# Three tiles in place of two for the pre-mix's input, and clearing split between VectorE and GpSimd

## The chip, the cores and the metric

The kernel runs on one core of one Trainium2 chip. The metric is device time in microseconds (us). One execution of the kernel before is profiled; times elsewhere are of separate runs. Engines are called PE (TensorE), ACT (ScalarE), DVE (VectorE), POOL (GpSimd) and SP (SyncE, which only issues transfers).

## The reference

Attention whose heads are mixed before and after the softmax, then two feed-forward layers, all in float32. 4 batches, 12 heads, 448 positions, 64 columns a head.

```python
scores = scale * np.matmul(q, k.transpose(0, 1, 3, 2))
scores = np.einsum('bhij,hg->bgij', scores, w_pre)       # pre-mix of the heads
scores = scores - np.max(scores, axis=-1, keepdims=True)
attn = np.exp(scores)
attn = attn / (np.sum(attn, axis=-1, keepdims=True) + 1e-09)
attn = np.einsum('bhij,hg->bgij', attn, w_post)          # post-mix
out = np.matmul(attn, v)
...
x = out.transpose(0, 2, 1, 3).reshape(B * S, H * D)      # 1792 x 768
x = elu(x @ moe_w_in) @ moe_w_out                        # 768 -> 2048 -> 768
h = x @ moe2_w_in                                        # 768 -> 1024
x = layernorm(h * softmax(h)) * g_ln @ moe2_w_out        # 1024 -> 768
```

## The kernel before

The attention goes through 17 chunks of query rows (`CH`, line 24). A chunk has G slots (4, 8, 12, 12, 9 in the first batch; 9 to 12 later), and a slot holds 10 query rows of all 12 heads. Two slots make a unit; there are 90.

For a chunk the steps are these. **Scores** (line 443): for each pair of heads PE multiplies queries by keys into PSUM tiles `sc`. **Eviction** (line 449): ACT or DVE copies each head's scores into an SBUF tile `sev` (8 buffers; `s` for chunk 0). **Moves** (lines 451 to 454): 13 DMAs bring the rows of the 12 heads into one tile `sp`, so that heads lie on partitions: head h of query row a on partition 13a + h. **Pre-mix** (line 510): one matmul of `wpre_t` with a slot of `sp` into `pm` (3 PSUM buffers, a unit uses two). Then follow for each unit the maximum on DVE (`st`, line 515), the exponential with its sum on ACT (`e`, 520), the division folded into the post-mix weights (`wr`, 531), the **post-mix** (`po`, 543), and its copy to `at` (551). When a chunk is complete, `av` (592) multiplies by the values, and the result goes to DRAM (`xs`).

`sp` has two tiles of 128 x 12 x 448 float32. They lie in the pools `spa` (right end of SBUF) and `spb` (left), and chunk c uses tile (17 - c) % 2. So the moves of chunk c wait until the pre-mix of chunk c-2 has read its last slot. Rows of the tile that no move writes must be zero, so both tiles are cleared whole at the start, one by DVE and one by POOL (line 470); DVE also clears the two PSUM tiles `po` (472), and POOL scales `wpre_t` (466).

The keys lie in a ring `k` of 12 buffers on the right side, behind `spa`; a batch needs 6. When the attention is near its end, `start_moe` (662) gives back `sev`, `q`, `kst`, `k` and `spa` and lays the tiles of the feed-forward layer there.

The order on every engine is made by a planner at build time. Each step is an `op` (287) with a rank (a due time in us), what it depends on, ring buffers that it takes (`bufs`, 284), and an estimated duration for each engine that may do it. `schedule` (296) simulates the engines: it takes the engine that could start first and, of the steps that it could then start, that with the lowest rank, and emits it. The engines run what they were given in order and wait on semaphores; SP, too, issues its transfers in order. `lag` is the time that the planner reckons from the end of a DMA's issue to the landing: 3.5 us for a move.

The due times: units' pre-mixes and post-mixes stand one behind the other from T0 = 14 us on (`plan_front`, lines 360 to 389). The scores of chunk c >= 2 are spread evenly between the first pre-mix of chunk c-1 (`lo`) and the first pre-mix of chunk c less SCM = 12 us (`hi`), lines 390 to 393. Steps on SP may be planned up to 4 us ahead of their rank (`AHS`), others up to 100 us (`AHD`). The moves of chunks 0 and 1 may be issued by SP or ACT, those of chunk 2 by SP or POOL, all others by SP.

The feed-forward layers behind (from line 725 on) are ordered by hand in their own loops and do not pass through the planner.

Of the kernel before, what the change touches and what calls it, by code (L numbers as in the profile page):

```python
# [9 lines left out]
F32 = mybir.dt.float32  # L10
# [4 lines left out]
ALU = mybir.AluOpType  # L15
# [3 lines left out]
NB, NH, S, D = 4, 12, 448, 64  # L19
# [4 lines left out]
CH = [(b, 10 * sum(n[:i]), n[i]) for b in range(NB) for n in [[[4, 8, 12, 12, 9], [11, 12, 12, 10], [12, 12, 12, 9], [11, 12, 12, 10]][b]] for i in range(len(n))]  # L24
NC = len(CH)
# [12 lines left out]
XB = 2  # L38
# [12 lines left out]
DB = .9  # L51
DA = .2
T0 = 14
SCM = 12
KD = 3.5
VD = 28
WB = 3
SB = 8
VB = 2
EB = 10  # L60
LEAD = 3

@with_exitstack
def kernel(ctx: ExitStack, tc: tile.TileContext, qa, kt, vt, wpre, wpost,
# [4 lines left out]
    nc = tc.nc  # L69
    ctx.enter_context(tc.manual_schedule())  # L70
    pools = {}

    def pool(name, bufs=1, side="left", space=None):
        kw = {"space": space} if space is not None else {"side": side}
        p = tc.alloc_tile_pool(name=name, bufs=bufs, reuse_waits="tile", **kw)
        pools[name] = p
        return p

    def release(*names):
        for n in names:  # L80
            pools.pop(n).release()
# [44 lines left out]
    wpre_t = const.tile([128, 64], F32, name="wpre_t")  # L126
    wpost_t = const.tile([128, 60], F32, name="wpost_t")

    pool("spa", 1, "right")
    k_p = pool("k", 12, "right")  # L130
    kst_p = pool("kst", 2, "right")
    q_p = pool("q", 4, "right")
    sev_p = pool("sev", SB, "right")
# [145 lines left out]
    class Op:  # L279
# [2 lines left out]
    ops = []  # L282
    tail = {"pe": .3, "act": .2, "dve": .17, "pool": .1, "sp": 2.0, "host": 0.0}
    bufs = {"sc": 3, "pm": 3, "po": 2, "sev": SB, "e": EB, "wr": WB, "st": 4, "kst": 2, "q": 4,
            "k": 12, "sp0": 1, "sp1": 1, "at": 2, "v": VB, "x": XB, "ws": 4, "wy": 2}

    def op(rank, emit, deps=(), new=(), uses=(), more=0.0, lag=None, **us):

        o = Op()
        o.rank, o.emit, o.deps, o.new, o.us, o.more, o.lag = rank, emit, [d for d in deps if d is not None], new, us, more, lag  # L290
        for b in chain(new, uses):
            b.users.append(o)
        ops.append(o)
        return o

    def schedule():
        free = dict.fromkeys(tail, 0.0)
        rings = {r: [] for r in bufs}
        todo = sorted(ops, key=lambda o: o.rank)

        def seen(o, e):

            if o.lag is not None:
                return o.end + o.lag
            if o.eng == e and e not in ("sp", "dve"):
                return o.end
            return o.end + tail[o.eng] + o.more

        def ready(o, e):
            t = 0.0  # L310
            for d in o.deps:
                if d.end is None:
                    return None
                t = max(t, seen(d, e))
            more = dict.fromkeys(bufs, 0)
            for b in o.new:
                ring = rings[b.ring]
                n = bufs[b.ring] - more[b.ring]
                more[b.ring] += 1
                if b.at is None and len(ring) >= n:  # L320
                    for u in ring[-n].users:
                        if u.end is None:
                            return None
                        t = max(t, seen(u, e))
            return t

        while todo:
            cand, start = [], {}
            for o in todo[:WIN]:
                opts = []  # L330
                for e, us in o.us.items():
                    r = ready(o, e)
                    if r is None:
                        break
                    r = max(r, o.rank - (AHS if e == "sp" else AHD))
                    opts.append((max(r, free[e]) + us + (DB if e == "dve" and "pool" in o.us and o.rank > TD else DA if e == "dve" and "act" in o.us else 0.0), r, e))
                else:
                    _, r, e = min(opts)
                    cand.append((o, e, r))
                    start[e] = min(start.get(e, 1e9), max(r, free[e]))  # L340
            e = min(start, key=start.get)
            o, _, r = min((c for c in cand if c[1] == e and c[2] <= start[e] + GRACE), key=lambda c: c[0].rank)
            o.eng = e
            t = max(r, free[e])
            o.end = free[e] = t + o.us[e]
            for b in o.new:
                if b.at is None:
                    b.at = o
                    rings[b.ring].append(b)
            o.emit(e)  # L350
            todo.remove(o)
        return max(free.values())
# [9 lines left out]
    t, nf, t_hid = T0, 0, None  # L362
# [32 lines left out]
    kt_t, kb, q_t, qb_, sp_t, sp_op, pre_op, e_t = {}, {}, {}, {}, {}, {}, {}, {}  # L395
# [3 lines left out]
    def dma(out, in_, e="sp"):  # L399
        {"act": nc.scalar, "pool": nc.gpsimd, "sp": nc.sync}[e].dma_start(out=out, in_=in_)  # L400
# [27 lines left out]
    def add_score(c, h):  # L428

        b, _, G = CH[c]  # L430
        n = 5 * G
        ring = ("sc", "pm")[h // 2 % 2] if c == 0 else "sc"
        scb, svb = [Buf(ring) for _ in range(2)], [Buf("sev") for _ in range(2)]
        r = t_sc[c, h]
        key = "sc", c, h

        def mm(e):
            T[key] = [pools["ps_" + ring].tile([128, 512], F32, tag=ring, name="sc") for _ in range(2)]
            q, k = q_t[c, h // 6], kt_t[b, h]
            for x in range(2):  # L440
                for i in range(2):
                    sl = slice(64 * i, 64 * i + 64)
                    nc.tensor.matmul(T[key][i][64 * x:64 * x + 64, :S], q[sl, h % 6 // 2, 64 * x:64 * x + 64], k[sl, :],  # L443
                                     start=True, stop=True)

        def evac(e, i):
            t = T["sv", c, h + i] = (k0.tile([128, S], F32, name=f"s0_{h + i}") if c == 0 else
                                     sev_p.tile([128, S], F32, tag="sev", name="sev"))
            copier(e)(t, T[key][i][:, :S])  # L449

        def move(e, i, p, r0, r1):
            if c not in sp_t:
                sp_t[c] = sp_t[c - 2]
            dma(sp_t[c][p:p + 13 * (r1 - r0 - 1) + 1:13, 0:G, :], T["sv", c, h + i][r0 * G:r1 * G], e)

        o1 = op(r, mm, [k_op[b, h], q_op[c, h // 6]], scb, [qb_[c, h // 6], kb[b, h]], pe=SC)
        for i in range(2):
            sv = [] if c == 0 else [svb[i]]
            o2 = sc_ev[c, h + i] = op(r + .9 + .1 * i, lambda e, i=i: evac(e, i), [o1], sv, [scb[i]], act=.43, dve=.54)
            for n, to in enumerate([(h + i, 0, 10)] if h + i < 11 else [(11, 0, 5), (64, 5, 10)]):  # L460
                sp_op.setdefault(c, []).append(op(r + 2 + .2 * i + .1 * n, lambda e, i=i, to=to: move(e, i, *to), [o2], [spb_[c]], sv, lag=3.5, sp=.78, **({"act": .78} if c < 2 else {"pool": 1.0} if c == 2 else {})))

    spb_ = {c: Buf(f"sp{(NC - c) % 2}") for c in range(NC)}
    o = op(7.0, lambda e: dma(wpre_t, wpre), sp=.5)
    o_wpost = op(T0 + 2, lambda e: dma(wpost_t, wpost), sp=.5)
    w_op = op(T0 - 8, lambda e: nc.gpsimd.tensor_scalar(wpre_t, wpre_t, 0.125, None, ALU.mult), [o], pool=.6)

    for c in range(2):
        sp_t[c] = pools["spb" if (NC - c) % 2 else "spa"].tile([128, NH, S], F32, tag="sp", name="sp")
        (nc.gpsimd if c else nc.vector).memset(sp_t[c], 0.0)  # L470
    for t in po_p:
        nc.vector.memset(t, 0.0)

    def begin(e):
        release("k0")
# [21 lines left out]
    for u, sl in enumerate(units):  # L497
# [62 lines left out]
        o = op(r0 + 3.2, guard, ex, [], [sb], dve=.07)  # L560
        o = op(r0 + 3.3, inv, [o], [], [sb], dve=.07)
        ow = op(r0 + 3.4, weigh, [o, o_wpost], [wb], [sb], dve=.3, pool=.38)
        r0 = t_post[u]
        o = op(r0, post, ex + [ow], pob, eb + [wb], pe=POST)
# [5 lines left out]
    for c in range(NC):  # L570
# [12 lines left out]
        for n in range(2):  # L583
            r = t_av[c, n]
# [10 lines left out]
            o = op(r, mm, at_ops[c] + ov, [avb], [vb, at_b[c]], pe=AV * w / 120)  # L595
# [10 lines left out]
            o = op(r + AV + .2, take, [o], [xb], [avb], act=.36, dve=.42)  # L606
# [4 lines left out]
    for n in range(16):  # L611
# [40 lines left out]
        o = op(t0, load, [last], [sb], sp=.5, lag=11.0)  # L652
        o = op(t0 + 4, clamp, [o], [], [sb], dve=.17)
        oa = op(t0 + 4.5, scale, [o], [], [sb], act=.26)
        o = op(t0 + 5, loword, [o], [], [sb], dve=.17)
        o = op(t0 + 5.5, sign, [o], [], [sb], dve=.27)
        o = op(t0 + 6, join, [oa, o], [], [sb], dve=.27)
# [3 lines left out]

    def start_moe(e):
        nonlocal gln_t
        release("sev", "q", "kst", "k", "spa")
        p = pool("wstg", 2, "right")
        gln_t = p.tile([128, F2 // 128], F32, name="gln_t", bufs=1)
        dma(gln_t, gln)
        w1_alloc(0, pool("w1a", 1, "right"))
        xT_alloc(0, pool("xT0", 1, "right"))
# [43 lines left out]
    for ft in range(2):  # L713
        o = None
# [3 lines left out]
    for i in range(3):  # L718
        ws = Buf("ws")
# [252 lines left out]
```

## Time and profile before

| | us |
|---|---|
| median of 3 runs | 1096.0 (1095.16 to 1097.95) |
| profiled execution, its time | 1094.9 |
| its span, first to last instruction | 1093.1 |
| PE busy in the span | 1059.9 (97%) |
| DVE, ACT, POOL busy | 722.0, 504.2, 231.6 |
| mean granted clock of PE | 0.998 |

The first pre-mix begins at 17.85 us and the last one at about 356 us; behind that comes the feed-forward part. Busy time of PE is an upper bound of its useful time, since ends of matmuls are modelled. What stands in brackets in a timeline row is the idle time of that engine just before, and what ended it.

### The profile page before, as it was taken

The numbers are of one execution on the slowest core, as the hardware profiler recorded it, in microseconds if no ns is written. First come the engines' busy times: TensorE is split into PE (matmuls) and PEld (weight loads), VectorE is DVE, ScalarE is ACT, GpSimd is POOL, SyncE is SP. The second block draws the span as 40 slices with busy tenths as digits, with TensorE's granted clock in tenths as the row PEclk, the third lists the DMA queues.
The fourth block names the chain that finished last, engine by engine and source line by source line (L and its number), as shares of the span: only waits on it lengthen the run. The fifth ranks groups of instructions, "written<-read, shape, count | busy, mean of one in ns | idle before, by whom it ended". The sixth has DMA issues, their size and how long they took to land.

```text
span 1093.1 us, 28427 instructions
## 1 busy us (share of the span) xinstructions
PE 1059.9 (97%) x11800; PEld 888.6 (81%) x11800; DVE 722.0 (66%) x1391; ACT 504.2 (46%) x1071; POOL 231.6 (21%) x243
## 2 busy tenths in 40 slices
PE   6899999999999999999999999999999999999998
PEld 2457667667666898998988999999999889898988
DVE  6576687677677557687887887878864644353522
ACT  3566676677676455333333443333431434342422
POOL 2211010011011325343343433343431000000000
PEclk9999999999999999999999999999999999999999
DMA  6875775775746442415234242423262400000001
GB/s 200 210 209 172 216 238 172 219 221 176 232 149 197 132 133 72 155 58 171 99 117 149 83 154 77 140 91 126 70 243 100 194 30 15 30 23 22 30 15 44
DMA packets 80287, 141.69 MB, mean 130 GB/s; under 512 B 20853, under 2 KB 59969, under 8 KB 80157
## 3 DMA queue, kind: packets, MB, share of 16 engines
q1 hardware_dynamic: 78345, 136.59, 39.1%
q10 hardware_dynamic: 1332, 2.09, 0.6%
q8 instruction: 93, 1.52, 0.6%
q0 software_dynamic: 480, 1.19, 0.4%
q14 instruction: 37, 0.30, 0.1%
HBM read 75.96 MB, written 25.17 MB: 93 GB/s over the span
## 4 chain that ended last, share of the span: by engine, by line
PE 74%; DMA 9%; DVE 8%; ACT 4%; issue 2%; SPq 1%; POOL 1%; ACTq 0%; DVEq 0%; POOLq 0%
PE h L256 15%; PE o L745 15%; PE o L888 11%; PE h L841 11%; PE av L592 6%; PE sc L443 5%; PE pm L510 5%; PE po L543 5%; DMA sp<-sev 3%; DMA ws<-in_wo_dram 2%; DVE x L761 1%; DVE wy L184 1%; DMA ws<-in_wi_dram 1%; PE tr L872 1%; DVE wq L180 1%
## 5 line engine op out<-in xcount | busy, mean ns | idle before, releaser
L520 ACT ACTIVATE e<-pm,st 128x448 f32<-128x448 f32 x180 | 113.4, 635 | 72.3 <-DVE st L515 65.9
L515 DVE TENSOR_REDUCE st<-pm 128x1 f32<-128x448 f32 x180 | 105.1, 617 | 60.9 <-PE pm L510 58.6
L745 PE MATMUL o<-gh,woh 128*128 128x448 f32 x384 | 141.3, 368 | 3.8 <-ACT x L759 1.9
L745 PE MATMUL o<-glo,woh 128*128 128x448 f32 x384 | 139.9, 364 | 0.0
L745 PE MATMUL o<-gh,wol 128*128 128x448 f32 x384 | 139.8, 364 | 0.0
L443 PE MATMUL sc<-kt,q 64*64 64x448 f32 x816 | 123.8, 565 | 9.7 <-ACT sev L449 4.6
L543 PEld LDWEIGHTS po<-wr,e 60*64 60x64 f32 x5040 | 102.4, 135 | 37.0 <-issue 23.8
L269 POOL TENSOR_TENSOR glo<-g,gh 128x448 fp32r<-128x448 f32 x64 | 83.1, 1298 | 217.9 <-issue 124.5
L510 PE MATMUL pm<-sp,wpre_t 64*64 64x448 f32 x720 | 112.2, 558 | 10.4 <-DMA xs<-x 4.4
L888 PE MATMUL o<-w,lh 128*128 128x384 f32 x448 | 120.3, 340 | 0.0
L543 PE MATMUL po<-wr,e 60*64 60x60 f32 x5040 | 109.1, 219 | 2.3 <-issue 1.1
L841 PE MATMUL h<-w,x2h 128*128 128x512 f32 x336 | 107.7, 395 | 0.0
L761 DVE TENSOR_TENSOR x<-x,o 128x448 f32<-128x448 f32 x168 | 101.4, 610 | 7.9 <-PE o L745 7.9
L256 PE MATMUL h<-xh,wih 128*128 128x448 f32 x288 | 105.5, 366 | 0.0
L256 PE MATMUL h<-xh,wil 128*128 128x448 f32 x288 | 105.0, 365 | 0.0
L256 PE MATMUL h<-xl,wih 128*128 128x448 f32 x288 | 104.9, 364 | 0.0
L264 ACT ACTIVATE t<-t 128x448 f32<-128x448 f32 x64 | 37.0, 578 | 134.7 <-DVE t L263 134.7
L531 POOL TENSOR_TENSOR wr<-wpost_t,st 128x120 f32<-128x120 f32 x90 | 36.3, 403 | 294.7 <-DVE st L527 225.7
L592 PEld LDWEIGHTS av<-at,v 128*64 128x64 f32 x1632 | 75.8, 137 | 14.1 <-DVE st L515 3.5
L592 PE MATMUL av<-at,v 128*64 128x120 f32 (+5 forms) x1632 | 83.2, 258 | 3.3 <-issue 1.8
L745 PEld LDWEIGHTS o<-gh,woh 128*128 128x128 f32 x384 | 72.1, 188 | 12.7 <-DVE x L761 4.5
L888 PEld LDWEIGHTS o<-w,lh 128*128 128x128 f32 x448 | 81.7, 188 | 0.6
(98 smaller groups left out, 1930.2 us busy)
## 6 DMA issues: line engine op xcount, KB each, us to landing
sp<-sev SPq DMA_DIRECT2D x94, 210.0 KB
ws<-in_wi_dram SPq DMA_DIRECT2D x33, 512.0 KB
ws<-in_wo_dram SPq DMA_DIRECT2D x21, 512.0 KB
q<-in_qa_dram SPq DMA_DIRECT2D x34, 192.0 KB
v<-in_vt_dram SPq DMA_DIRECT2D x24, 256.0 KB
w2s<-ws SPq DMA_DIRECT2D x12, 512.0 KB
ws<-in_wo_dram SPq DMA_DIRECT2D x16, 384.0 KB
w2s<-ws SPq DMA_DIRECT2D x16, 384.0 KB
```

The source lines that it names most:

```text
L256: nc.tensor.matmul(ps[:, :S], a[:, kc * FG + ft * 128:kc * FG + (ft + 1) * 128], x[:, kc, :], start=kc == 0 and n == 0, stop=kc == ECH - 1 ...
L269: nc.gpsimd.tensor_tensor(glo, g, f(gh), ALU.subtract)
L443: nc.tensor.matmul(T[key][i][64 * x:64 * x + 64, :S], q[sl, h % 6 // 2, 64 * x:64 * x + 64], k[sl, :], start=True, stop=True)
L510: nc.tensor.matmul(ps_t[u][r][64 * s:64 * s + 64, :S], wpre_t[p, :], sp_t[c][p, g, :], start=True, stop=True)
L515: nc.vector.tensor_reduce(out=st_t[u][:P, r:r + 1], in_=ps_t[u][r][:P, :S], op=ALU.max, axis=AX.X, negate=True)
L520: nc.scalar.activation(out=t[:P], in_=ps_t[u][r][:P, :S], func=AF.Exp, bias=st[:P, r:r + 1], scale=1.0, accum_out=st[:P, 2 + r:3 + r])
L543: nc.tensor.matmul(out[:, :, 5 * r:5 * r + 5], e_t[u, r][sl, 64 * n:64 * n + 64], wr_t[u][sl, r].rearrange("p (g a) -> p g a", a=5), start ...
L592: nc.tensor.matmul(ps[64 * k:64 * k + 64, i, :], v_t[CH[c][0]][:, 6 * n + 2 * i + k, q, :], at_t[c][:, q, 6 * n + 2 * i + k, :w], start=q ...
L745: nc.tensor.matmul(ps[:, :S], a[:, ft * DM + e * 128:ft * DM + (e + 1) * 128], x, start=n == 0, stop=n == 5)
L761: nc.vector.tensor_tensor(x1[tb][:, e, :], x1[tb][:, e, :], ps[:, :S], ALU.add)
L841: nc.tensor.matmul(ps[:, hf * 512:hf * 512 + 512], a[:, k, :], w, start=n == 0, stop=n == 3 * ECH - 1)
L888: nc.tensor.matmul(ps[:, :384], a[:, k, :], w, start=n == 0, stop=n == 3 * FC - 1)
```

## The change

A third tile for `sp` in a pool `spc` beside `spa`: chunk c uses tile (17 - c) % 3, and its moves wait for the last pre-mix of chunk c-3. To make room, the ring of keys has 8 buffers instead of 12. SCM, the lead of the scores, goes from 12 to 18 us. The moves of chunk 2 may be issued by SP or ACT, not by POOL; the planner's landing lag of moves becomes 5.0 us from chunk 2 on.

Of each of the first three tiles only the slots that chunks 0, 1 and 2 use are cleared ahead of everything (4 by DVE, 8 and 12 by POOL). The other slots of the first two tiles (8 and 4) are cleared by POOL behind that, as steps of the planner, and the moves of chunks 3 and 4 depend on them. The clears of the two `po` tiles become planner steps on DVE, and the scaling of `wpre_t` goes from POOL to DVE. The planner's POOL begins free at 8.0 us and its DVE at 3.5 us.

```diff
-SCM = 12
+SCM = 18
+KB = 8
...
     pool("spa", 1, "right")
-    k_p = pool("k", 12, "right")
+    pool("spc", 1, "right")
+    k_p = pool("k", KB, "right")
...
-            "k": 12, "sp0": 1, "sp1": 1, "at": 2, "v": VB, "x": XB, "ws": 4, "wy": 2}
+            "k": KB, "sp0": 1, "sp1": 1, "sp2": 1, "at": 2, "v": VB, "x": XB, "ws": 4, "wy": 2}
...
         free = dict.fromkeys(tail, 0.0)
+        free["pool"], free["dve"] = 8.0, 3.5
...
-                sp_t[c] = sp_t[c - 2]
+                sp_t[c] = sp_t[c - 3]
...
-                sp_op.setdefault(c, []).append(op(r + 2 + .2 * i + .1 * n, lambda e, i=i, to=to: move(e, i, *to), [o2], [spb_[c]], sv, lag=3.5, sp=.78, **({"act": .78} if c < 2 else {"pool": 1.0} if c == 2 else {})))
+                sp_op.setdefault(c, []).append(op(r + 2 + .2 * i + .1 * n, lambda e, i=i, to=to: move(e, i, *to), [o2, o_clear.get(c)], [spb_[c]], sv, lag=3.5 if c < 2 else 5.0, sp=.78, **({"act": .78} if c < 3 else {})))
...
-    spb_ = {c: Buf(f"sp{(NC - c) % 2}") for c in range(NC)}
-    o = op(7.0, lambda e: dma(wpre_t, wpre), sp=.5)
+    spb_ = {c: Buf(f"sp{(NC - c) % 3}") for c in range(NC)}
+    o = op(7.0, lambda e: dma(wpre_t, wpre), sp=.5, lag=7.0)
...
-    w_op = op(T0 - 8, lambda e: nc.gpsimd.tensor_scalar(wpre_t, wpre_t, 0.125, None, ALU.mult), [o], pool=.6)
-    for c in range(2):
-        sp_t[c] = pools["spb" if (NC - c) % 2 else "spa"].tile([128, NH, S], F32, tag="sp", name="sp")
-        (nc.gpsimd if c else nc.vector).memset(sp_t[c], 0.0)
+    w_op = op(T0 - 4, lambda e: nc.vector.tensor_scalar(wpre_t, wpre_t, 0.125, None, ALU.mult), [o], dve=.15)
+    for c in range(3):
+        sp_t[c] = pools["spa spb spc".split()[(NC - c) % 3]].tile([128, NH, S], F32, tag="sp", name="sp")
+        (nc.gpsimd if c else nc.vector).memset(sp_t[c][:, :CH[c][2]], 0.0)
+    def clear(t, us, r):
+        return op(r, lambda e: nc.gpsimd.memset(t, 0.0), pool=us)
     for t in po_p:
-        nc.vector.memset(t, 0.0)
+        op(T0 + 2, lambda e, t=t: nc.vector.memset(t, 0.0), dve=.49)
+    o_clear = {c + 3: clear(sp_t[c][:, CH[c][2]:], .38 * (NH - CH[c][2]), 4.0 + c) for c in range(2)}
...
-        release("sev", "q", "kst", "k", "spa")
+        release("sev", "q", "kst", "k", "spc", "spa")
```

## Rows read from the trace of the kernel before

**Rows 1.** Windows: a stretch, its length, busy time of engines, clock, DMA share, GB/s.
```profile
0.00:18.00 18.00, 11.09 (x73) 3.71 (x77) 10.30 (x11) 5.44 (x9) 5.16 (x6) 1.00 0.56 187
18.00:60.00 42.00, 36.13 (x745) 20.26 (x738) 26.24 (x60) 21.76 (x56) 6.86 (x14) 0.96 0.77 211
60.00:345.00 285.00, 273.73 (x6791) 191.96 (x6788) 205.99 (x521) 191.38 (x513) 30.00 (x77) 1.00 0.66 197
345.00:1093.10 748.10, 738.90 (x4207) 672.63 (x4206) 479.43 (x801) 285.60 (x495) 189.63 (x146) 1.00 0.29 98
```
**Rows 2.** Groups by line, 0 to 345 us: busy, mean ns; idle before, releasers.
```profile
L443 PE MATMUL sc<-kt,q 64*64 64x448 f32 x816 | 123.8, 565 | 9.7 <-ACT sev L449 4.6 <-DMA kt<-in_kt_dram 4.2 <-DVE s L449 0.8
L510 PE MATMUL pm<-sp,wpre_t 64*64 64x448 f32 x693 | 107.5, 558 | 10.2 <-DMA xs<-x 4.4 <-DMA sp<-sev 4.1 <-DMA q<-in_qa_dram 1.1
```
**Rows 3.** Groups by line on PE, 60 to 345 us.
```profile
L510 PE MATMUL pm<-sp,wpre_t 64*64 64x448 f32 x621 | 93.3, 553 | 6.6 <-DMA xs<-x 4.4 <-DMA q<-in_qa_dram 1.1 <-DMA sp<-sev 1.0
```
**Rows 4.** Timeline of PE: start, duration, instruction, idle time before it.
```profile
31.89 0.96 PE L510 MATMUL pm<-sp,wpre_t 64*64 64x448 f32 x2 [1.32 <-DMA sp<-sev]
33.74 0.90 PE L510 MATMUL pm<-sp,wpre_t 64*64 64x448 f32 x3 [0.89 <-DMA sp<-sev]
...
50.74 0.98 PE L510 MATMUL pm<-sp,wpre_t 64*64 64x448 f32 x8 [0.82 <-DMA sp<-sev]
...
71.60 0.93 PE L510 MATMUL pm<-sp,wpre_t 64*64 64x448 f32 x2 [1.93 <-DMA xs<-x]
...
133.81 1.00 PE L510 MATMUL pm<-sp,wpre_t 64*64 64x448 f32 x5 [1.34 <-DMA xs<-x]
```
**Rows 5.** Windows, the stretch with the lower clock.
```profile
33.96:37.37 3.41, 3.41 (x20) 1.22 (x18) 1.57 (x3) 1.18 (x4) 0.00 (x0) 0.51 0.93 195
```
**Rows 6.** Timeline of SP's queue, moves of chunks 3 and 6.
```profile
46.85 3.40 SPq L400 DMA_DIRECT2D sp<-sev  x4
...
112.25 3.59 SPq L400 DMA_DIRECT2D sp<-sev  x4
...
126.12 2.43 SPq L400 DMA_DIRECT2D sp<-sev  x3
```
**Rows 7.** Timeline of PE, the last pre-mixes of chunks 1 and 4.
```profile
45.09 0.93 PE L510 MATMUL pm<-sp,wpre_t 64*64 64x448 f32 x7
...
100.63 1.20 PE L510 MATMUL pm<-sp,wpre_t 64*64 64x448 f32 x8
```
**Rows 8.** Instructions on the tile sp: ns minimum/median/maximum, first and last start.
```profile
L400 SPq DMA_DIRECT2D sp<-sev x194: 721/756/1861, 18.9 to 335.8; - x194
L400 ACTq DMA_DIRECT2D sp<-sev x8: 784/786/800, 15.1 to 26.5; - x8
...
DMA to landing us min/median/max: 7.2/8.1/9.5
```
**Rows 9.** Timeline of 0 to 24 us.
```profile
0.74 4.58 POOL L470 MEMSET sp<- 128x5376 f32 x1 [0.29 <-POOLq L961]
...
1.94 4.54 DVE L470 MEMSET sp<- 128x5376 f32 x1 [1.94 <-issue]
...
6.05 0.53 ACT L449 COPY s<-sc 128x448 f32<-128x448 f32 x1 [2.61 <-PE sc L443]
6.58 1.02 DVE L472 MEMSET po<- 128x512 f32 x2
...
7.51 1.13 DVE L449 COPY s<-sc 128x448 f32<-128x448 f32 x2
...
9.16 0.37 POOL L466 TENSOR_SCALAR wpre_t<-wpre_t 128x64 f32<-128x64 f32 x1 [3.83 <-DMA wpre_t<-in_wpre_dram]
...
22.98 0.63 DVE L449 COPY sev<-sc 128x448 f32<-128x448 f32 x1
...
23.15 0.39 POOL L531 TENSOR_TENSOR wr<-wpost_t,st 128x120 f32<-128x120 f32 x1 [13.62 <-DVE st L527]
```
**Rows 10.** Waits of DVE, 0 to 345 us: total, times, longest.
```profile
DVE sev L449 <- DMA v<-in_vt_dram: 2.5, 1, 2.5
```

## The prediction

> **What bounds the kernel now.** I read the stages first, then TensorE's (PE's) idle time by line, then its gaps one by one, then the queues that feed it. The table by stage [rows 1] shows PE busy 1059.9 of 1093.1 us, so all that a better order can win is 33.2 us of idle time. Of this, 9.2 us lie behind 345 us, in the two feed-forward layers, which the change doesn't touch. Before that stand 6.9 us up to 18 us, 5.9 us from 18 to 60 us, and 11.3 us from 60 to 345 us. The first 4.2 us are the wait for the first key tile, which stays. So at most some 20 us (1.8%) are within reach.
>
> By line [rows 2], the idle time ahead of the pre-mix matmul is 10.2 us up to 345 us, and nearly all is charged to DMAs: 4.4 + 4.1 + 1.1 = 9.6 us. The labels differ (`xs`, `sp`, `q`), but the pre-mix reads only `sp` and `wpre_t`, and SP issues all of these transfers; I read all three as the landing of the chunk's moves. Scores come second: 9.7 us, of which 4.2 us are the first key tile and 4.6 us an eviction on ACT. From 60 us on [rows 3] the pre-mix's share is 6.6 us, 6.5 of it behind DMAs. The gaps [rows 4] stand at first pre-mixes of chunks: 1.32 and, in the same unit, 0.89 us at chunk 1, 0.82 at chunk 2, 1.93 at chunk 3, 1.34 at chunk 6. After the gap at chunk 1 the granted clock falls to its lower level: 0.51 over 3.41 us [rows 5], which is 1.2 of 2.4 GHz, so about 1.7 us are lost there as well.
>
> Two things can make the moves late. One is the tile: with two, chunk c's moves wait for the last pre-mix of chunk c-2. Chunk 1's last pre-mix begins at 45.09 us and chunk 3's first move is issued in the row at 46.85 us [rows 6, 7]: there the tile binds. The other is the order: chunk 4's last pre-mix stands at 100.63 us, so chunk 6's tile is free from about 102 us, but its moves run only from 112.25 to 128.55 us [rows 6, 7], and PE still waits 1.34 us. There it is the due times that are late.
>
> **The change, part by part.** *Order.* By the plan's own constants, a chunk of 12 slots lasts 6 x (0.76 + 0.83) + 4.56 + 5.2 = 19.3 us, so with SCM = 12 the six score pairs are spread over 7.3 us from the first pre-mix of the chunk before; with 18 they are due within 1.3 us of it. After a chunk of 9 or 10 slots (chunks 5, 9, 13) they are due 5.5 to 7.1 us before it, and there only a third tile lets the moves follow. 13 moves need 13 x 0.756 = 9.8 us of SP [rows 8], against the 16.3 us that chunk 6's took; landing takes 128.55 to 133.81 us, 5.3 us, on SP, and 8.1 us in the median of POOL's. So up to some 6 us earlier landing stand against gaps of 0.5 to 1.93 us. From 60 us on: between 0 (the other loads in SP's queue eat the advance) and 6.5 us; I take 5, since the advance is longer than any gap, but some chunks have 10 to 13 us between first pre-mixes, hardly more than the issues and a landing. The lag of 5.0 instead of 3.5 works the same way: the plan puts other matmuls ahead of a pre-mix whose data it holds to be later. It is in the same term.
>
> *Chunk 2.* Its POOL moves go to SP or ACT. Its gap is 0.82 us: 0 to 0.8, I take 0.8. Up to 13 issues of 0.79 us on ACT [rows 8] are hidden by ACT's idle time; if they aren't, the exponentials behind them are late (in the bunching, below).
>
> *Chunk 1.* Its due times stay, and it never waited for a tile. Its gaps are 2.2 us, and with the clock 3.9 us hang on them. What helps is only an earlier chunk 0 and chunk 2's scores, due 6 us earlier, as a filler. 0 to 3.9 us; I take 0.9, near the lower end.
>
> *Clearing.* DVE clears 4 slots instead of 12: 4.54 x 4/12 = 1.5 us, from 1.94 to 3.45 us, and the two `po` clears (1.02 us) can run until 4.5 us, ahead of the first score. Before, they held DVE until its first eviction at 7.51 us, while ACT's first began at 6.05 us [rows 9]. This frees 0 (if the landing of keys sets the pace) to 1.46 us; I take 0.7. POOL now clears 8, 12, 8 and 4 slots: 32/12 x 4.58 = 12.2 us, from 0.74 to about 13 us. Its next work was at 23.15 us, and chunk 3's moves, which newly wait for the clear, came at 46.85 us: hidden by 10 and by 30 us, cost nothing. Behind that wait would stand SP's whole queue (queries, keys, stores), and so PE; but it is over long before. Scaling `wpre_t` moves to DVE, 0.37 us if it takes as long there as on POOL. It waits for its load (landed by 9.16 us, where POOL's began [rows 9]): if it stood at 6 us in DVE's queue, the evictions behind it would lose 3 us. The plan's lag of 7.0 puts it behind that; I take nothing.
>
> One rule of the skill speaks against this part. The rows first: DVE's eviction at 22.98 us took 0.63 us with POOL's multiply at 23.15 us inside it (0.39 us), and the two clears side by side took 4.54 and 4.58 us [rows 9], so neither pair held the other up. The Trainium skill (SBUF — State Buffer, "Who interferes with whom") says that DVE and GpSimd share a port pair that a copy in a two-port mode can take, and that the later of the two is then blocked for the whole instruction. By these rows the rule doesn't bite; by the rule, a clear could block evictions. That is rival E.
>
> *Keys.* 12 buffers become 8, a batch needs 6: four of a new batch's six loads wait for scores of the old batch's last chunk, which are now due some 19 us (or one chunk) before the new ones are needed. SP waits in order, so a load that came up too early would hold moves. Zero, up to 1 us at each of three batches; it goes into the next term.
>
> *Bunching, a cost.* Twelve evictions (0.53 on ACT, 0.62 on DVE) now crowd at each chunk's start, before reductions and exponentials that PE's next units need. The nearest rows are the waits of scores for evictions, 4.6 + 0.8 = 5.4 us [rows 2]. From 0 to 14 us (1 us at each of 14 chunks); I take 1.4, a quarter more than these waits, since the plan fills PE with whatever else is ready.
>
> *Memory and tail.* The wider stack on the right moves what later lies there. The late stage has its own order and the release waits for the same chunk 15 as before: nothing either way.
>
> The sum: 5 + 0.8 + 0.9 + 0.7 - 1.4 = 6.0 us. The profiled execution took 1094.9 us (span 1093.1 and 1.8 around it), so 1088.9; it lies 1.1 us under the median of the runs, from which 6.0 gives 1090.0. I say 1089.5.
>
> **Rivals.** *A, nothing moves.* The moves come no earlier, because SP's queue with its loads and the 16 DMA engines (share 0.66 from 60 to 345 us [rows 1]) set their pace, or the gaps go from one chunk to the next. For: chunk 6 had its tile 10 us early and was late. Against: its moves took 16.3 us where issues need 9.8. Gains of 0.7 + 0.8 and costs of 1.4 cancel: about 1095.
>
> *B, slower.* Scores come in a bunch of twelve, but there are 8 `sev` buffers; the ninth eviction waits until the first move has landed, 5.3 to 8.1 us after its issue where the plan reckons with 5.0. An ACT or DVE that stands before such an eviction keeps exponentials or maxima behind it, and with three `pm` buffers PE stops a unit later. At 1 us in each of chunks 3 to 16 this is 14 us against gains of 7.4: 1094.9 - 7.4 + 14 = 1101.5. It decides from 7.4/14 = 0.53 us per chunk. For: the ring isn't made larger. Against: with a worse lag of 3.5, the longest wait of DVE's evictions for a DMA up to 345 us is one of 2.5 us [rows 10].
>
> *C, more.* All DMA gaps go (9.6), the clock doesn't fall (1.7), the front wins 1.46, with no bunching: 12.8 us, 1082.
>
> *E, the shared port.* POOL's clears hold DVE's six evictions of chunk 0. From 3.8 to 13 us a POOL clear is always running, of up to 4.58 us each; one block of that length costs the front about 4.6 us less what ACT takes over: 1094.9 - 6.0 + 4.6 = 1093.5.
>
> **How the numbers follow.** A difference under 0.3% (3.3 us) can't be told from none here. The forecast (3.3 to 10 us faster) has 0.52, C 0.10, A 0.20, E 0.05, B 0.13. Faster: 0.52 + 0.10 = 0.62; same: 0.20 + 0.05 = 0.25; slower: 0.13. The likeliest case by itself spans 1085 to 1092.7. As slower and faster cases both count, the range goes from 1081 (C) to 1099, which leaves the worse half of B and the extremes of C outside.
>
> **What would show it.** Right: the pre-mix's idle time behind DMAs falls from 9.6 to 2 or 3 us; moves of chunks 5, 9 and 13 begin before the last pre-mix of chunks 3, 7 and 11; DVE's first eviction begins near 6 us; the first pre-mix near 17 us. A shows in moves that begin and end where they did. B shows as `sev` evictions on ACT or DVE that wait for DMAs and as new PE gaps behind exponentials. E shows as evictions on DVE far over 0.62 us before 13 us. I am wrong most likely if the waits simply go on to evictions (B), or if the front is set by chunk 1's landing, with the low clock in the same place.

## The result, and the profile after

The changed kernel takes 1084.82 us in the median (1079.4 to 1087.23, 7 runs) against 1095.16 us before (1091.4 to 1098.44, 7 runs). The ratio is 0.9904, 95% interval 0.9879 to 0.993: faster by 10.3 us. 1089.5 us was predicted, 1081 to 1099 the range, so the direction was right and the forecast gain too small by 4 us (6.0 for 10.3). The profiled execution has a span of 1077.6 us and was itself the quickest of the seven (1079.4 us), so differences between the two profiles (15.5 us) overstate the gain by half.

The stages of the changed kernel, in the columns of [rows 1] (the last stretch is shorter by what was won before it):

```profile
0.00:18.00 18.00, 11.50 (x74) 3.88 (x78) 8.80 (x13) 4.91 (x8) 12.37 (x8) 0.91 0.64 209
18.00:60.00 42.00, 35.82 (x741) 19.85 (x735) 27.23 (x62) 21.59 (x58) 3.11 (x8) 1.00 0.70 205
60.00:345.00 285.00, 280.56 (x7144) 200.28 (x7138) 216.55 (x544) 202.86 (x539) 40.03 (x84) 1.00 0.71 210
345.00:1077.60 732.60, 725.00 (x3854) 662.57 (x3854) 466.66 (x777) 273.04 (x466) 185.21 (x141) 1.00 0.28 95
```

Against [rows 1] nothing is won up to 60 us: PE is idle for 6.5 and 6.2 us there, before for 6.9 and 5.9. From 60 to 345 us the idle time falls from 11.3 to 4.4 us. The groups on PE, first up to 345 us and then, after the dots, from 60 us on, answer to [rows 2, 3]:

```profile
L446 PE MATMUL sc<-kt,q 64*64 64x448 f32 x816 | 119.5, 560 | 8.9 <-DMA kt<-in_kt_dram 4.0 <-ACT sev L452 3.8 <-DVE s L452 1.0
L518 PE MATMUL pm<-sp,wpre_t 64*64 64x448 f32 x720 | 108.6, 556 | 5.0 <-ACT e L528 4.2 <-DMA v<-in_vt_dram 0.6 <-issue 0.2
...
L518 PE MATMUL pm<-sp,wpre_t 64*64 64x448 f32 x648 | 94.6, 555 | 1.4 <-ACT e L528 0.7 <-DMA v<-in_vt_dram 0.6
```

The pre-mix waited 9.6 us for DMAs before; now it waits 0.6. New are 4.2 us of waits for exponentials, 3.5 of them in the first 60 us; before, these were 0.3 us. The same two kinds of matmul were busy for 123.8 us [rows 2] and 112.2 us in all before:

```profile
L510 PE MATMUL pm<-sp,wpre_t 64*64 64x448 f32 x720 | 112.2, 558 | 10.4 <-DMA xs<-x 4.4
```

Here the same 816 and 720 take 119.5 and 108.6 us. PE's busy time as a whole fell from 1059.9 to 1052.9 us. So 7.0 of the 15.5 us between the two profiles were busy time, not idle time.

The front, as a timeline (start, duration, instruction, idle time before it), beside [rows 9]:

```profile
0.73 7.61 POOL L473 MEMSET sp<- 128x3584 f32 x2 [0.29 <-POOLq L969]
...
1.18 1.55 DVE L473 MEMSET sp<- 128x1792 f32 x1 [1.18 <-PEq L969]
...
5.90 0.62 DVE L452 COPY s<-sc 128x448 f32<-128x448 f32 x1 [2.04 <-PE sc L446]
...
8.27 4.62 POOL L476 MEMSET sp<- 128x3584 f32 x2
...
12.02 0.92 DVE L469 TENSOR_SCALAR wpre_t<-wpre_t 128x64 f32<-128x64 f32 x1
...
17.18 0.97 PE L518 MATMUL pm<-sp,wpre_t 64*64 64x448 f32 x1
...
31.79 1.29 PE L518 MATMUL pm<-sp,wpre_t 64*64 64x448 f32 x5 [0.16 <-issue]
```

DVE's first eviction comes at 5.90 instead of 7.51 us, and the first pre-mix at 17.18 us, 0.67 us earlier. At chunk 1's first pre-mix that is gone: 31.79 against 31.89 us [rows 4]. The stretch at the lower clock (0.50, 1.2 of 2.4 GHz) didn't go either. It only moved ahead, to the scores and first pre-mixes from 14.90 us on, behind gaps of PE of 1.03 and 0.80 us:

```profile
14.90:18.30 3.40, 2.80 (x16) 1.04 (x12) 0.62 (x1) 0.53 (x1) 0.00 (x0) 0.50 0.65 188
```

### The profile page after: what moved, and what is told of

Its sections match the earlier page's. It is cut to its first block, busy times and chain, and to the rows that moved or that the text cites. A ratio compares the mean times of both kernels' runs of the same rounds, so it can differ in the third digit from the quotient of the medians.

```text
span 1077.6 us, 28434 instructions
## 1 busy us (share of the span) xinstructions
PE 1052.9 (98%) x11800; PEld 886.6 (82%) x11800; DVE 719.2 (67%) x1394; ACT 502.4 (47%) x1068; POOL 240.7 (22%) x240
## 4 chain that ended last, share of the span: by engine, by line
PE 78%; DVE 9%; DMA 6%; ACT 3%; issue 3%; SPq 1%; POOL 1%; ACTq 0%; DVEq 0%; POOLq 0%
PE h L258 15%; PE o L753 15%; PE o L896 11%; PE h L849 11%; PE av L600 6%; PE po L551 6%; PE pm L518 6%; PE sc L446 6%; DMA ws<-in_wo_dram 2%; DVE x L769 1%; DMA sp<-sev 1%; DVE wy L186 1%; DMA ws<-in_wi_dram 1%; PE tr L880 1%; DVE wq L182 1%
## 5 line engine op out<-in xcount | busy, mean ns | idle before, releaser
L446 PE MATMUL sc<-kt,q 64*64 64x448 f32 x816 | 119.5, 560 | 8.9 <-DMA kt<-in_kt_dram 4.0
L518 PE MATMUL pm<-sp,wpre_t 64*64 64x448 f32 x720 | 108.6, 556 | 5.0 <-ACT e L528 4.2
L539 POOL TENSOR_TENSOR wr<-wpost_t,st 128x120 f32<-128x120 f32 x88 | 34.1, 388 | 283.8 <-DVE st L535 228.0
```

The costliest lines, as they stand in the source:

```text
L518: nc.tensor.matmul(ps_t[u][r][64 * s:64 * s + 64, :S], wpre_t[p, :], sp_t[c][p, g, :], start=True, stop=True)
```

## The experiments

All ratios are to the kernel before, run beside them on the same chip (its medians were 1093.2 us for the first four and 1093.7 us for the others), with 95% intervals. The theory at the outset (T) was that of the prediction: the third tile and the longer lead of the scores work together. SCM is one number, but more than the scores hang on it: the planner counts the due times of the queries' loads, of the evictions and of the moves from those of the scores.

**Taking the change apart.** First the lead back to 12, all else as changed:

```diff
-SCM = 18
+SCM = 12
```

> The changed kernel with SCM back at 12; third tile, 8 key buffers, landing lag 5.0 and the split clearing stay. Theory T (tile and lead work together: the third tile only pays where the scores come early enough to use it, so most of the gain is at chunks 5, 9 and 13): with SCM 12 the pre-mix's idle time behind DMAs comes back to 4 us or more from 60 us on, and the time is 1088 to 1092, so a third to two thirds of the 10 us gain is lost. Rival U (the third tile alone does it): 1085, no loss. Rival L (any new order may win or lose some us): no relation, also slower than before is possible.

1089.87 us, ratio 0.9964 (0.9939 to 0.9988): about two thirds of the gain is gone. From 60 us on the waits for moves are partly back (3.8 us behind DMAs, where it was 6.5 before the change and T said 4 or more):

```profile
L518 PE MATMUL pm<-sp,wpre_t 64*64 64x448 f32 x628 | 94.4, 555 | 5.0 <-DMA sp<-sev 3.5 <-issue 1.1 <-DMA v<-in_vt_dram 0.3
```

So three tiles, eight keys, the split clearing, chunk 2's moves on SP and ACT and the landing lag of 5.0 together give 3 to 4 us at this lead. Then the lead alone, in the kernel before:

```diff
-SCM = 12
+SCM = 18
```

> The kernel before with SCM = 18 alone; two tiles, 12 key buffers, lag 3.5, whole clears. Theory T: chunks 6 and 14, whose tile was free early, gain 1 to 2 us; chunks 5, 9 and 13 can't begin their moves before the last pre-mix of chunks 3, 7, 11: 1091 to 1095. Rival D (due times alone do it): 1085.

1084.3 us, ratio 0.9918 (0.9883 to 0.9954). One number makes, within the intervals, the whole gain. T falls here, and D (what counts is when the scores are due) takes its place. Its pre-mixes from 60 us on:

```profile
L510 PE MATMUL pm<-sp,wpre_t 64*64 64x448 f32 x640 | 96.5, 554 | 2.3 <-DMA xs<-x 1.0 <-DMA kt<-in_kt_dram 0.5 <-DMA sp<-sev 0.5
```

The front was taken out of the changed kernel, and put alone into the kernel before:

```diff
-        free["pool"], free["dve"] = 8.0, 3.5
...
-    w_op = op(T0 - 4, lambda e: nc.vector.tensor_scalar(wpre_t, wpre_t, 0.125, None, ALU.mult), [o], dve=.15)
+    w_op = op(T0 - 8, lambda e: nc.gpsimd.tensor_scalar(wpre_t, wpre_t, 0.125, None, ALU.mult), [o], pool=.6)
...
-        (nc.gpsimd if c else nc.vector).memset(sp_t[c][:, :CH[c][2]], 0.0)
+        (nc.gpsimd if c else nc.vector).memset(sp_t[c], 0.0)
...
     for t in po_p:
-        op(T0 + 2, lambda e, t=t: nc.vector.memset(t, 0.0), dve=.49)
-    o_clear = {c + 3: clear(sp_t[c][:, CH[c][2]:], .38 * (NH - CH[c][2]), 4.0 + c) for c in range(2)}
+        nc.vector.memset(t, 0.0)
```

> The changed kernel without its front: three tiles cleared whole ahead of everything (one by DVE, two by POOL), the two po clears at once on DVE, the scaling of wpre_t on POOL, both planner engines free at 0. Theory T: the front was worth 0.7 us, so 1085 to 1086.5, if POOL's clears (two of 4.6 us, done by 10 us) are hidden. Rival F (the front is worth several us because later stages follow it): 1088 or more.

1082.82 us, ratio 0.9894 (0.9853 to 0.9934): no loss without it, and under T's 1085 to 1086.5.

> The kernel before with the front alone: two tiles, of each only the slots that chunks 0 and 1 use cleared first, the others by POOL behind, po clears and wpre_t as planner steps on DVE; SCM 12, lag 3.5 and 12 key buffers as before. Theory T: 0 to 1 us faster than before (1094 to 1095). Rival F: 3 us or more faster.

(The lines above the other way round, with two tiles.) 1093.72 us, ratio 0.9999 (0.9971 to 1.0026): no gain with it. The split clearing is worth nothing that can be measured.

**How much lead, and does the tile matter at more of it?** Three values of SCM for two tiles or three, each a change of that one line:

> The kernel before with SCM = 15 alone (two tiles, 12 key buffers). Theory D (what counts is when the last scores of a chunk are due, since the last move's landing decides the first pre-mix; the tile count doesn't matter at this lead): half of the way between SCM 12 and 18, ratio to before about 0.996, with the pre-mix's idle time behind DMAs from 60 us on between 2 and 5 us. Rival L (18 is a lucky order, another value may land anywhere): ratio anywhere from 0.99 to 1.01, with no relation to those waits.

> The kernel before with SCM = 24 alone (two tiles, 12 key buffers); scores are now due up to 13 us ahead of the first pre-mix of the chunk before. Theory D: the waits for moves are gone already at 18, the moves can't begin before the tile is free, so no more gain: ratio 0.989 to 0.994. Rival G (each us of lead pays on): ratio under 0.985. Rival B of the prediction (scores that crowd in ahead of their tile fill the 8 sev buffers and hold evictions): ratio over 0.997.

> The changed kernel with SCM = 24. If the third tile has a value, it shows where two tiles can't follow the lead. Theory D: nothing more to win, ratio to before 0.987 to 0.993, like the changed kernel and like two tiles at 24. Rival T2 (the third tile pays at a longer lead): at least 4 us under two tiles at SCM 24.

| SCM | two tiles | three tiles, with the rest of the change |
|---|---|---|
| 12 | 1 (the kernel before) | 0.9964 (0.9939 to 0.9988) |
| 15 | 0.9935 (0.9915 to 0.9956) | |
| 18 | 0.9918 (0.9883 to 0.9954) | 0.9904 (0.9879 to 0.993) |
| 24 | 1.006 (1.0032 to 1.0088) | 0.9942 (0.992 to 0.9964) |

At 15 most of the gain is there, more than the half that D said, and the pre-mix waits 0.1 us from 60 us on. At 24 two tiles lose, which D had excluded, and three tiles, with the rest of the change, are 13.6 us better than two, as T2 said, but not better than 18. The loss of two tiles has two places. One is the front: PE takes chunk 2's scores ahead of chunk 1's work, stands for their queries, and chunk 1's first pre-mix comes at 49.66 us instead of 31.89 (with three tiles at this lead it comes at 42.65 us):

```profile
39.38 4.13 PE L443 MATMUL sc<-kt,q 64*64 64x448 f32 x18 [3.58 <-DMA q<-in_qa_dram]
43.81 0.98 PE L443 MATMUL sc<-kt,q 64*64 64x448 f32 x6 [0.30 <-ACT sev L449]
49.66 1.47 PE L510 MATMUL pm<-sp,wpre_t 64*64 64x448 f32 x8 [3.35 <-issue]
```

The other is rival B of the prediction. From 60 us on evictions stand for moves that can't leave their `sev` buffers, on ACT (total, times, longest):

```profile
ACT sev L449 <- DMA sp<-sev: 5.5, 6, 2.4
```

With three tiles at the same lead ACT has no such wait there, and DVE's fall from 5.7 to 2.2 us. To part the two places, the lead of 24 was given to chunks 3 to 16 only:

```diff
-    lo, hi = (t_pre[first[c - 1]], t_pre[first[c]] - SCM) if c > 1 else (T0 - 5, T0 - 1) if c else (2, T0 - 6)
+    lo, hi = (t_pre[first[c - 1]], t_pre[first[c]] - (24 if c > 2 else 12)) if c > 1 else (T0 - 5, T0 - 1) if c else (2, T0 - 6)
```

> The kernel before with a lead of 24 us for chunks 3 to 16 and of 12 for chunk 2. Theory D with the loss of two tiles at SCM 24 put on the front (chunk 2's scores pushed ahead of chunk 1's work: chunk 1's first pre-mix at 49.7 us instead of 31.9): that comes back to 31 to 33 us, and the ratio is 0.988 to 0.995. Rival B (evictions held by full sev buffers cost the late chunks): it stays at 1.000 or above.

1091.93 us, ratio 0.9986 (0.9963 to 1.0009). Chunk 1's first pre-mix is back at 30.7 us, and 9 us of the median with it, but no gain over SCM 12 is left; up to 345 us ACT's evictions wait 9.5 us for moves, in 9 places. D's 0.988 to 0.995 is missed, and the interval just reaches B's 1.000. That the full `sev` buffers take the gain is read from these waits; a larger ring of them wasn't tried.

> The changed kernel with a lead of 24 us for chunks 3 to 16 and of 12 for chunk 2. Theory D: the pre-mix waits for nothing at 18 either, so the ratio stays at 0.987 to 0.993. Rival T2 (the third tile pays at a longer lead): 3 us or more under two tiles with the same leads, and under 0.987.

1087.16 us, ratio 0.993 (0.9911 to 0.9948). Three tiles, with the rest of the change, are worth 5 us here, as T2 said, but its 0.987 isn't reached, and against 18 nothing is won: the pre-mix waits 0.1 us, and a new wait has come, for the loads of the queries:

```profile
PE sc L446 <- DMA q<-in_qa_dram: 6.0, 3, 2.8
```

**The parts that remain.** Keys: `KB = 12` in the changed kernel.

> The changed kernel with the ring of keys back at 12 buffers (three tiles as well). If 8 keys cost something that the third tile wins back, this is faster than the changed kernel: rival K, ratio to before 0.985 or less. Theory D: the key loads have a chunk's time to spare, ratio 0.988 to 0.993.

1084.8 us, ratio 0.9913 (0.9882 to 0.9943): eight keys cost nothing. And the tile alone out of the changed kernel:

```diff
-    pool("spc", 1, "right")
...
-                sp_t[c] = sp_t[c - 3]
+                sp_t[c] = sp_t[c - 2]
...
-    spb_ = {c: Buf(f"sp{(NC - c) % 3}") for c in range(NC)}
+    spb_ = {c: Buf(f"sp{(NC - c) % 2}") for c in range(NC)}
...
-    for c in range(3):
+    for c in range(2):
...
-    o_clear = {c + 3: clear(sp_t[c][:, CH[c][2]:], .38 * (NH - CH[c][2]), 4.0 + c) for c in range(2)}
+    o_clear = {c + 2: clear(sp_t[c][:, CH[c][2]:], .38 * (NH - CH[c][2]), 4.0 + c) for c in range(2)}
```

> The changed kernel with two tiles and nothing else undone: SCM 18, lag 5.0, 8 key buffers, split clearing (the other slots of the two tiles now for chunks 2 and 3). Theory D (the lead of the scores made the gain): ratio to before 0.989 to 0.994, equal to the changed kernel. Rival T (the third tile made it): 0.997 or more.

1081.41 us, ratio 0.9874 (0.9847 to 0.9901). That is the best median of all, a little under D's 0.989; its interval overlaps that of the changed kernel. At SCM 18 the third tile brings nothing that can be measured. Five kernels have this lead (the changed one, the kernel before with the lead alone, and those without the front, with twelve keys and with two tiles); they lie between 0.9874 and 0.9918, so the gain isn't the luck of one order.

The traces show why. These are the moves of chunk 6 in SP's queue, first in the changed kernel (its first four are the last four in the row of eight, from 101.12 us on; its last three are the first three in the row at 118.28 us):

```profile
97.52 7.82 SPq L403 DMA_DIRECT2D sp<-sev  x8
...
109.06 1.65 SPq L403 DMA_DIRECT2D sp<-sev  x2
...
113.85 3.77 SPq L403 DMA_DIRECT2D sp<-sev  x4
...
118.28 4.21 SPq L403 DMA_DIRECT2D sp<-sev  x5
```

and then with two tiles:

```profile
106.73 7.02 SPq L402 DMA_DIRECT2D sp<-sev  x8
...
114.69 2.25 SPq L402 DMA_DIRECT2D sp<-sev  x2
...
117.65 2.43 SPq L402 DMA_DIRECT2D sp<-sev  x3
```

With three tiles the moves begin 5.6 us earlier (101.12 and 106.73 us), and with two they wait and then go eight in a row. But in both the last one is issued at about 120 us (118.28 + three of 0.84 = 120.8; 117.65 + 2.43 = 120.1), because it stands behind the last scores, which PE ends at 116.2 and at 114.5 us, and it is the last move that lets the first pre-mix go. That begins at 128.31 us with three tiles and at 126.54 us with two, with no idle time before it:

```profile
128.31 1.20 PE L518 MATMUL pm<-sp,wpre_t 64*64 64x448 f32 x8
...
126.54 0.91 PE L517 MATMUL pm<-sp,wpre_t 64*64 64x448 f32 x5
```

Chunk 6 is no exception. In chunks 3 to 16 the last move's issue ends 2.7 to 5.9 us behind the chunk's last score with three tiles, and 2.9 to 5.9 us with two. In the kernel before, PE ended chunk 6's scores at 123.1 us, and the last move's issue ended at 128.55 us [rows 6].

**A shorter lead.** If each us of lead counts, fewer must cost:

```diff
-SCM = 12
+SCM = 8
```

> The kernel before with SCM = 8 alone, so the scores of a chunk are due 4 us later than before. Theory D: the pre-mix's idle time behind DMAs from 60 us on rises from 6.5 us to 12 us or more, and the ratio to before is 1.005 to 1.015. Rival L (12 was an unlucky order, any other is better): 0.995 or less.

1093.2 us, ratio 0.9989 (0.9966 to 1.0012): no loss. From 60 us on the pre-mix waits 3.3 us for moves, not 12; the rest of these waits now stands before that, at chunks 1 and 2. Up to 345 us they are 9.8 us, much as in the kernel before (9.6):

```profile
L510 PE MATMUL pm<-sp,wpre_t 64*64 64x448 f32 x688 | 102.7, 563 | 11.6 <-DMA sp<-sev 9.8 <-issue 1.3 <-ACT e L520 0.3
```

So waits and time agree, but 4 us less of lead didn't lengthen either. Here D failed. L isn't borne out either, since this order is no better than 12.

## Why the prediction came out

**The number.** The gain of 10.3 us lies just past the forecast's 3.3 to 10 us and short of C's 12.8, so the range held. That the sum came near is partly luck. The waits for moves went as forecast, but the terms of chunk 1 and of the clearing (0.9 and 0.7 us) brought nothing that the runs show, the third tile wasn't needed, and a fall of busy time that no term names came on top.

**Right.** The forecast of the gaps. From 60 us on 5 of the 6.5 us behind DMAs were to go; 5.9 went. Chunk 2's 0.82 us went. The first pre-mix came 0.67 us earlier (0.7 said), and DVE's first eviction at 5.90 us (near 6 said). Eight keys, the clears on POOL and the scaling on DVE cost nothing in the time.

**Wrong in its bound.** "All that a better order can win is 33.2 us of idle time" is a step that failed: the sum prices idle time alone. Of the 15.5 us between the profiles 8.5 are idle time and 7.0 are busy time, against 6.0 forecast. One pre-mix unit has eight matmuls of 0.536 us (the median) which overlap: all eight take 0.98 us in the row at 50.74 us [rows 4]. Where the data of some are late, a few run by themselves: at 71.60 us two took 0.93 us, and at 73.03 us three more 0.60 us, in one unit:

```profile
73.03 0.60 PE L510 MATMUL pm<-sp,wpre_t 64*64 64x448 f32 x3 [0.50 <-DMA sp<-sev]
```

That counts as busy. A count over all matmul records of the attention bears it out: the time in which fewer than four of them ran at once fell from 32.7 to 24.9 us, and the time with four or more stayed (309.7 and 310.5). The first pre-mix units of the 17 chunks were busy for 25.3 us in the kernel before, 20.3 in the changed one, and 25.5 with SCM 8, which gained nothing. How much busy time goes differs between executions: in the changed kernel with twelve keys, at a mean granted clock of 0.994 instead of 0.998, PE was busy for 1059.1 us, 0.8 under the kernel before.

**Mis-sized.** Bunching was to cost 1.4 us, by waits for evictions and for exponentials. At SCM 18 scores wait 4.8 us for evictions up to 345 us, where it was 5.4: there it costs nothing. The exponentials were held up, though: the pre-mix's waits for them rose from 0.3 to 4.2 us, where 1.4 was taken for the whole term. The lead alone doesn't do that: in the kernel before with SCM 18 the pre-mix has no such wait. So the rest of the change has a part in it, perhaps ACT's issuing of chunk 2's moves; no run parts that. At 24 with two tiles bunching does show, as evictions that wait for moves, and no gain is left.

**Wrong in its cause.** "There only a third tile lets the moves follow", for chunks 5, 9 and 13, made the tile a condition of the gain. Without it the gain is the same (0.9874 and 0.9918 beside 0.9904). "It is the due times that are late", said of chunk 6, described the general case, but the reading under it was wrong. The row at 100.63 us isn't chunk 4's last pre-mix [rows 7]. Chunk 4 has nine slots, and the ninth shares a unit with chunk 5's first:

```profile
111.18 0.98 PE L510 MATMUL pm<-sp,wpre_t 64*64 64x448 f32 x8
```

The matmuls on chunk 4's slot end at 111.79 us, and chunk 6's first move is issued at 112.25 us: the tile was free 0.5 us early, not 10. In 8 of chunks 3 to 16 of the kernel before, the first move's issue begins within 0.5 us of the tile's last read. So the rows of before spoke for the tile, and only the runs could tell: in the kernel of 1081.41 us, with two tiles, it is 10 of 14 chunks, and the pre-mix waits for no move.

The check named for the forecast, that moves of chunks 5, 9 and 13 begin before the last pre-mix of chunks 3, 7 and 11, came true (85.24, 163.77 and 244.81 us against 89.99, 168.52 and 249.12). It says nothing about the time, since the first move isn't the one that is waited for.

**Chunk 1.** Of 3.9 us on its gap and the clock 0.9 were taken. The gap went (0.16 us left), but chunk 1 began no earlier: up to 60 us the 3.0 us behind moves went, and 3.2 more behind exponentials came. The low clock stayed, in another place. So nothing came of it.

**Rivals.** A fell for the change as a whole; that nothing is won is true of the front by itself, and of the tile at the lead of 18. B's loss shows with two tiles at a lead of 24. C had the moves' waits nearly right: all but 0.6 us went. A's ground that chunk 6 had its tile 10 us early falls with the misread row. E's lock was seen (below), but not on evictions, and at a place that cost nothing.

**Open.** Why SCM 8 loses nothing. A due time is only a priority in this planner, and PE takes scores earlier when it has nothing else, which may be why a shorter lead changes little; no run tells that apart. And whether the landing lag of 5.0 does something: the changed kernel with two tiles (0.9874) differs from SCM 18 alone (0.9918) by that lag too, but the intervals overlap, and the lag wasn't tried alone. Nor is it known which part gives the 3 to 4 us at SCM 12: the tile, the lag and chunk 2's moves weren't parted there.

## What to carry to other kernels

Before a buffer is added, ask which transfer of the group is waited for. A further buffer lets the first transfer go earlier; the consumer waits for the last one, and that one may hang on the producer's place in the order, which costs no memory to move. Take changes apart even when they win: here one constant carries the gain, and at that lead a third tile, a smaller ring and a split clear added nothing that could be measured. And idle time isn't all that an order can win where short matmuls overlap, because the ones that run by themselves look busy.

## What was not expected of the hardware

DVE's scaling of `wpre_t`, 64 elements a partition, took 0.92 us in the changed kernel, from 12.02 to 12.94 us. POOL's clear ran until 12.89 us. In the changed kernel with SCM 12 the same instruction began later beside the same clear and ended at the same time; in the kernel before with the front alone, POOL's clears were over at 8.38 us:

```profile
8.27 4.62 POOL L476 MEMSET sp<- 128x3584 f32 x2
...
12.42 0.52 DVE L469 TENSOR_SCALAR wpre_t<-wpre_t 128x64 f32<-128x64 f32 x1
```

```profile
3.77 4.61 POOL L474 MEMSET sp<- 128x3584 f32 x2
...
11.92 0.18 DVE L467 TENSOR_SCALAR wpre_t<-wpre_t 128x64 f32<-128x64 f32 x1
```

0.92, 0.52 and 0.18 us, and the two long ones end within 0.05 us of the end of the clear. In three more kernels with three tiles (SCM 24, lead 24 from chunk 3 on, twelve keys) it began at 12.13, 11.68 and 11.66 us and ended at 12.94 us each time; with two tiles and SCM 18, where the clears were over early, it took 0.18 us. DVE's evictions from PSUM beside the same clears kept their 0.62 us, and the one after the scaling waited for PE, so the block cost nothing. The Trainium skill (SBUF — State Buffer, "Who interferes with whom") says that a copy or tensor_scalar in a two-port mode on DVE shares its ports with GpSimd and that the later one is blocked for the whole instruction. These rows agree with it for the tensor_scalar from SBUF to SBUF. The prediction had set the rule aside on rows of another kind, evictions and clears.
